# A retention layer and two gated MLPs on one core: block 0's sixteen steps in a written order, state products in four quarters, weights read back permuted

## The chip, the core and the metric

The kernel runs on one core of one Trainium2 chip. The metric is device time of one execution in microseconds (us), as the median of several runs. TensorE does the matmuls, VectorE, ScalarE and GpSimd the elementwise work, SyncE issues the transfers. In the profile they are PE, DVE, ACT, POOL and SP, and PEld is the loading of weights into TensorE. All matmuls of this kernel write PSUM, which is organised in banks of 512 fp32 columns for each partition.

## The reference

Three stages follow each other. A retention layer (batch 2, 8 heads, 768 positions, head size 64) keeps one 64x64 state for each head. Its output, as 1536 tokens of 512 features, goes through a gated MLP with 2048 hidden features, and then through a normalised second MLP with 1536. Weights and inputs are given in double precision.

```python
def _attn_ref(q, k, v):
    gamma = 1.0 - 2.0 ** (-5.0 - np.arange(H, dtype=np.float32))
    for t in range(S):
        state = gamma[None, :, None, None] * state + np.einsum('bhd,bhe->bhde', k[:, :, t], v[:, :, t])
        y[:, :, t] = scale * np.einsum('bhd,bhde->bhe', q[:, :, t], state)

def _moe_ref(x, w_in, w_out):
    h = x @ w_in
    g = h * (1.0 / (1.0 + np.exp(-1.702 * h)))
    return g @ w_out

def _moe2_ref(x, w_gate, w_val, w_out, rms_g):
    rms = np.sqrt(np.mean(x * x, axis=-1, keepdims=True) + 1e-06)
    xn = x / rms * rms_g
    g = xn @ w_gate
    silu = g * (1.0 / (1.0 + np.exp(-g)))
    val = xn @ w_val
    return silu * val @ w_out
```

## The kernel before

**Tokens and blocks.** The 1536 tokens are three blocks of 512, each of four chunks of 128 positions, so the retention layer has twelve chunks, 0 to 11, with a new batch at chunk 6. An opening computes chunks 0 to 3, which are the tokens of block 0. Then a loop of sixteen steps f runs the first MLP for block 0, 128 hidden features a step, and fits the retention of chunks 4 to 11 between. After it, blocks 1 and 2 go through the first MLP together, by seven products for each pair of steps in the manner of Strassen (`m0` to `m7`, L712), and the second MLP follows.

**A weight's way.** A weight tile w arrives as double words. One conversion turns it into fp32: two ScalarE copies (L162, L163), and on VectorE a shift (L166), a sum on 16-bit words (L167) and the sign (L173), each needing the one before. Every matmul operand of the MLPs is split into a high half (a rounded copy on ScalarE, L387 or L420) and a low half (the difference, on VectorE, L388 or L421), and a product is three matmuls. The names end in h and l: `wih`, `wil` for the input weights, `gh`, `gl` for the gate; `wo` holds both halves of an output weight. Converted input weights are also stored to memory (`wm0d` and so on, two steps in a tile), output weights as halves (`wo0d`), and `reload` (L189) reads the former back for blocks 1 and 2, 512 KB in one transfer.

**A step.** Step f does the twelve matmuls of h (L405, `mlp1_in`), one visit to the retention, the gate g (L427, L420, L421) and the twelve matmuls `acc` of step f-1 (L382 to L384). Visits alternate between scores (L265) with their two masks (L277, VectorE) and the state visit. Steps 4 and 9 have two visits. A state visit has the inter products (L294: the state S_sb times the decayed queries, skipped where a batch begins), the intra products (L307: masked scores times values), the copy of y to x, called xr (L328, ScalarE), and, unless the batch ends, the update products u (L351) with the decay (L359, ScalarE) and the sum (L367, VectorE) of the state. Inter puts head 2n+e at rows e of the array and at partitions e of one PSUM tile y, so two of the array's four 64x64 quarters are used.

**What sets the order.** Up to the end of the opening the order of each engine is the written one (`in_order(opening)`). From there a scheduler places each engine's instructions by priority, under data dependencies; only the instructions of the first two steps (`HELD`) are kept behind the opening's last one on their engine. Loads of weights, stores and reloads go by SyncE in its order. At the end of the loop the work of blocks 1 and 2 starts: sums and splits of x (`m_tasks`, L579 and L388: `xm`, `xml`, `mt`) and of weight set 0 and 1 (`set_tasks`, L612: `swm`, parts x, y, z), placed at steps 13 to 15.

Of the kernel before, what the change touches and what calls it, by code (L numbers as in the profile page):

```python
# [18 lines left out]
C = 128  # L19
# [19 lines left out]
HELD = 2  # L39
# [6 lines left out]
def tile_retention_mlp_swiglu(  # L46
# [146 lines left out]
    def split_in(f):  # L193
        if f < F1:
            t = parts["wi", f] = [wa_p.tile([128, 512], F32R, tag=f"wa{s}", name=f"wi{s}{f}") for s in "hl"]
            halves(*t, raw["w1", f][:, 0:512].bitcast(F32))
# [4 lines left out]
    def split_out(f):  # L201
        t = wo_p.tile([128, 1024], F32R, tag="wo", name=f"wo{f}")
        parts["wo", f] = both(t)
        halves(*both(t), raw["w1", f][:, 512:1024].bitcast(F32))
# [133 lines left out]
    def attend(c, p):  # L338
        inter(c, p)
        intra(c)  # L340
        x_high(c)
        at.pop(("y", c))
# [42 lines left out]

    def halves(hi, lo, src):
        nc.scalar.activation(out=hi, in_=src, func=ACTF.Copy)  # L387
        nc.vector.tensor_tensor(out=lo, in0=src, in1=hi.bitcast(F32), op=ALU.subtract)  # L388
# [29 lines left out]
    def gate_parts(key, g):  # L418
        hi, lo = gt[key] = two_parts(key[1])
        nc.scalar.activation(out=hi, in_=g, func=ACTF.Copy, scale=1.0 / GELU)  # L420
        nc.vector.scalar_tensor_tensor(  # L421
# [3 lines left out]
    def mlp1_act(f, ps):  # L425
        g = tmp(f"g{f}")
        nc.scalar.activation(out=g, in_=ps, func=ACTF.Silu, scale=GELU)  # L427
        gate_parts(("wo", f), g)
# [447 lines left out]
    ends = in_order(opening)  # L876

    def attention(c):
        return [lambda: scores(c, ps_t), lambda: (attend(c, ps_t), state(c, ps_t), following(c))]
# [8 lines left out]
    def next_of(tasks):  # L888
        if tasks:
            tasks.pop(0)()  # L890

    att = [x for c in range(CPB, B * NC) for x in attention(c)]
# [305 lines left out]
```

## Time and profile before

| what | value |
|---|---|
| median of 3 runs | 596.02 us (595.58 to 596.24) |
| the profiled execution's own time | 594.39 us |
| its span in the trace | 592.6 us |
| TensorE busy | 584.7 us, 99% |
| VectorE busy | 450.5 us, 76% |
| ScalarE busy | 357.3 us, 60% |
| GpSimd busy | 26.1 us, 4% |
| granted TensorE clock | 1.00 in every stretch shown |

The profiled execution is one run, and its time stands beside the median. The span is what the trace covers between its first and last instruction. A busy share is an average over the whole span; what bounds a stretch is read from the timelines of that stretch. In the rows, `y<-qd,S_sb` says which tile is written from which; in square brackets stands how long the engine stood idle before an instruction, and what it then had been waiting for. Matmul records overlap, so their starts are compared and not their durations.

### The profile page before, as it was taken

What the parts mean: (1) busy time and instruction counts of PE and PEld (TensorE: products, weight loads), DVE (VectorE), ACT (ScalarE), POOL (GpSimd) and SP (SyncE); (2) the same over time, 40 slices, a digit from 0 to 9 for tenths busy, and PEclk for the clock granted to TensorE, in tenths of its full rate; (3) what the DMA queues carried; (4) which work ended last, traced back from release to release, by engine and by line L of the source; (5) the groups of instructions that cost most, each with busy time, mean ns of one, the idle gap of its engine ahead of it and who ended that gap; (6) DMA issues with size and microseconds to landing.
All of it is one profiled execution on the core that took longest, in us unless ns stands there. A gap on an engine that the chain in (4) does not pass through costs nothing.

```text
span 592.6 us, 9365 instructions
## 1 busy us (share of the span) xinstructions
PE 584.7 (99%) x3306; PEld 486.2 (82%) x3306; DVE 450.5 (76%) x828; ACT 357.3 (60%) x684; POOL 26.1 (4%) x28
## 2 busy tenths in 40 slices
PE   9999999999999999999999999999999999999997
PEld 6787887887788888878878888888989889988885
DVE  2999897978999786647889999987765766654542
ACT  2686767865777786536458676555554445544532
POOL 4300311000000000000000000000000000000000
PEclk9999999999999999999999999999999999999999
DMA  8989899898269888987894644736223376553521
GB/s 328 395 237 414 334 314 364 290 310 301 75 247 308 300 284 303 287 292 266 291 341 133 194 140 143 267 107 205 98 90 106 101 266 239 177 158 103 167 72 71
DMA packets 47855, 135.11 MB, mean 228 GB/s; under 512 B 5568, under 2 KB 5824, under 8 KB 47808
## 3 DMA queue, kind: packets, MB, share of 16 engines
q1 hardware_dynamic: 47376, 134.37, 66.4%
q8 instruction: 26, 0.43, 0.3%
q10 hardware_dynamic: 432, 0.14, 0.1%
q14 instruction: 21, 0.17, 0.1%
HBM read 98.84 MB, written 35.65 MB: 227 GB/s over the span
## 4 chain that ended last, share of the span: by engine, by line
PE 90%; DMA 5%; DVE 2%; ACT 2%; SPq 0%; issue 0%
PE acc L382 7%; PE h L405 7%; PE acc L384 7%; PE acc L383 6%; PE o L382 6%; PE o L383 6%; PE o L384 6%; DMA w<-in_w 2%; PE sc L265 1%; PE y L307 1%; PE y L294 1%; DMA qk<-in_qk 1%; DMA wowq<-wo11d 1%; PE g2a L712 1%; PE v2a L712 1%; PE g10a L712 1%
## 5 line engine op out<-in xcount | busy, mean ns | idle before, releaser
L383 PE MATMUL o<-w,gh 128*128 128x512 f32 x144 | 56.2, 390 | 0.0
L384 PE MATMUL o<-w,gl 128*128 128x512 f32 x144 | 56.1, 389 | 0.0
L382 PE MATMUL o<-w,gh 128*128 128x512 f32 x144 | 55.7, 390 | 0.0
L167 DVE CUSTOM_DVE_ANT_0 qw<-qw,uw 128x1024 uint16<-128x1024 uint16 x68 | 48.2, 710 | 2.9 <-ACT uw L163 0.5
L162 ACT ACTIVATE qw<-w 128x512 f32<-128x512 f32 x68 | 45.0, 662 | 0.7 <-DMA w<-in_w 0.7
L163 ACT ACTIVATE uw<-w 128x512 uint32<-128x512 uint32 x68 | 45.3, 666 | 0.0
L166 DVE TENSOR_SCALAR qw<-qw 128x512 uint32<-128x512 uint32 x68 | 30.7, 452 | 18.2 <-ACT qw L162 18.2
L388 DVE TENSOR_TENSOR gl<-gw,gh 128x512 fp32r<-128x512 f32 x24 | 16.6, 692 | 25.7 <-ACT gh L387 25.7
L384 PEld LDWEIGHTS o<-w,gl 128*128 128x128 f32 x144 | 27.0, 188 | 5.6
L387 ACT ACTIVATE gh<-gw 128x512 fp32r<-128x512 f32 x24 | 15.1, 631 | 27.3 <-PE o L383 24.6
L382 PEld LDWEIGHTS o<-w,gh 128*128 128x128 f32 x144 | 27.1, 188 | 4.7
L383 PEld LDWEIGHTS o<-w,gh 128*128 128x128 f32 x144 | 27.1, 188 | 4.6
L382 PE MATMUL acc<-gh,wo 128*128 128x512 f32 x64 | 26.0, 411 | 0.0
L382 PE MATMUL acc<-gh,wowq 128*128 128x512 f32 x64 | 25.2, 394 | 0.6 <-ACT x L448 0.5
L382 PE MATMUL acc<-gh,wowp 128*128 128x512 f32 x64 | 24.3, 393 | 1.2 <-ACT gh L420 1.2
L384 PE MATMUL acc<-gh,wowq 128*128 128x512 f32 x64 | 25.2, 394 | 0.0
L384 PE MATMUL acc<-gh,wo 128*128 128x512 f32 x64 | 25.1, 393 | 0.0
L383 PE MATMUL acc<-gl,wo 128*128 128x512 f32 x64 | 25.1, 393 | 0.0
L383 PE MATMUL acc<-gl,wowq 128*128 128x512 f32 x64 | 25.0, 391 | 0.0
L383 PE MATMUL acc<-gl,wowp 128*128 128x512 f32 x64 | 25.0, 390 | 0.0
L384 PE MATMUL acc<-gh,wowp 128*128 128x512 f32 x64 | 24.9, 389 | 0.0
L173 DVE SCALAR_TENSOR_TENSOR qw<-w,qw 128x512 uint32<-128x512 uint32 x36 | 24.6, 684 | 0.1
(1510 smaller groups left out, 1695.9 us busy)
## 6 DMA issues: line engine op xcount, KB each, us to landing
w<-in_w SPq DMA_DIRECT2D x68, 512.0 KB, 5.7
qk<-in_qk SPq DMA_DIRECT2D x12, 512.0 KB, 8.1
kv<-in_kv SPq DMA_DIRECT2D x12, 512.0 KB, 8.4
gmd<-gm SPq DMA_DIRECT2D x16, 256.0 KB, 4.0
gwm<-gmd SPq DMA_DIRECT2D x16, 256.0 KB, 4.0
g1d<-gs SPq DMA_DIRECT2D x12, 256.0 KB, 2.4
g2d<-gl SPq DMA_DIRECT2D x12, 256.0 KB, 2.0
gw<-g1d SPq DMA_DIRECT2D x12, 256.0 KB, 2.7
```

The costliest lines, as they stand in the source:

```text
L162: nc.scalar.activation(out=q, in_=high.bitcast(F32), func=ACTF.Copy, scale=2.0 ** -112)
L163: nc.scalar.activation(out=t, in_=low, func=ACTF.Copy, scale=2.0 ** -29)
L166: lambda: nc.vector.tensor_scalar(out=m, in0=m, scalar1=3, scalar2=None, op0=ALU.logical_shift_left),
L167: lambda: nc.vector.tensor_tensor(out=m, in0=m, in1=t, op=ALU.add),
L173: nc.vector.scalar_tensor_tensor(out=dst, in0=high, scalar=0x80000000, in1=m, op0=ALU.bitwise_and, op1=ALU.bitwise_or)
L382: nc.tensor.matmul(out=out, lhsT=ah, rhs=bh, start=first, stop=False)
L383: nc.tensor.matmul(out=out, lhsT=ah, rhs=bl, start=False, stop=False)
L384: nc.tensor.matmul(out=out, lhsT=al, rhs=bh, start=False, stop=last)
L387: nc.scalar.activation(out=hi, in_=src, func=ACTF.Copy)
L388: nc.vector.tensor_tensor(out=lo, in0=src, in1=hi.bitcast(F32), op=ALU.subtract)
L405: nc.tensor.matmul(out=ps, lhsT=w[a][:, k * 128:(k + 1) * 128], rhs=x[b][:, k, :], start=o == order[0], stop=o == order[-1])
L712: nc.tensor.matmul(out=bank, lhsT=u, rhs=v, start=first and k == 0 and x == 0, stop=k == 1 and x == 2, skip_group_check=True,)
```

## The change

Four things change. First, the sixteen steps are written out in an order for all four compute engines, and that order is held to the end of the loop (`in_order(opening)` stands behind it). Of the two conversions that each step carries, the first is done inside the step; of the second, the ScalarE part stands at the end of a step and the VectorE part at the start of the next. High and low halves are issued apart (`in_high`, `in_low` and so on), and masks and state sums have written places. Second, the state visits of chunks 4 to 11 put head 2n+e at rows e and columns n%2 of the array, with the two e in two PSUM banks, `y_0` and `y_1`, so all four quarters are used; `u` moves to the other PSUM pool; the copy to x becomes two copies, `x_raw`. Third, this leaves the features of x in another order for blocks 1 and 2, so `reload` reads their input weights back in that order, as eight transfers of 64 KB, each with pieces of 512 bytes, where one of 512 KB stood. Fourth, set 0 is read back at step 11 instead of 13, and a table, `AHEAD`, says how many of the sums and splits of x and of set 0 each late step takes.

```diff
--- before.py
+++ after.py
-HELD = 2
+AHEAD = {F1 - 7: (1, 0), F1 - 5: (1, 0), F1 - 3: (0, 2), F1 - 2: (2, 2), F1 - 1: (3, 1)}
...
     def reload(kind, i):
         t = raw[kind, i] = wr_p.tile([128, 1024], F32, tag="wr", name=f"{kind}{i}r")
-        nc.sync.dma_start(out=t, in_=kept[kind, i])
+        if kind != "wm":
+            nc.sync.dma_start(out=t, in_=kept[kind, i])
+            return
+        to = t.rearrange("p (f e i c) -> p f e i c", f=2, e=2, i=2)
+        of = kept[kind, i].rearrange("p (f i s c) -> p f i s c", f=2, i=2, s=2)
+        for f in range(2):
+            for s in range(2):
+                for e in range(2):
+                    nc.sync.dma_start(
+                        out=to[64 * s:64 * s + 64, f, e], in_=of[64 * e:64 * e + 64, f, :, s]
+                    )
...
     def attend(c, p):
-        inter(c, p)
-        intra(c)
-        x_high(c)
-        at.pop(("y", c))
+
+        y = [psum(p, f"y{c}_{e}") for e in range(2)]
+        at_of = lambda n, e: y[e][64 * (n % 2):64 * (n % 2) + 64, n // 2 * C:n // 2 * C + C]
+        if c % NC:
+            qd = at.pop(("qd", c))
+            for n in range(NP):
+                for e in range(2):
+                    r = slice(64 * e, 64 * e + 64)
+                    nc.tensor.matmul(
+                        out=at_of(n, e),
+                        lhsT=S_two[(c - 1) % 2][r, n, :],
+                        rhs=qd[r, n * C:(n + 1) * C],
...
+        for e in range(2):
+            for n in range(NP):
+                nc.tensor.matmul(
+                    out=at_of(n, e),
+                    lhsT=ld["kv", c][:, 1, 2 * n + e, :],
+                    rhs=at["a", c, e][:, n * C:(n + 1) * C],
...
+    def x_raw(c):
+        for e, y in enumerate(at.pop(("y", c))):
+            nc.scalar.activation(
+                out=x_of(c)[0][:, 2 * e:2 * e + 2], in_=y[:, 0:2 * C].rearrange("p (i t) -> p i t", i=2), func=ACTF.Copy
+            )
...
-    ends = in_order(opening)
...
+    visits = deque(x for c in range(CPB, B * NC) for x in (("scores", c), ("state", c)))
+
+    def visit(what, c):
+
+        if what == "scores":
+            score_products(c, ps_t)
+            return [], [lambda: masks(c)]
+        attend(c, ps_t)
+        last = c % NC == NC - 1
+        if not last:
+            update_products(c, ps_h)
+        following(c)
+        if last:
+            return [lambda: x_raw(c)], []
+        return [lambda: x_raw(c)], [lambda: decay(c), lambda: add_update(c)]
...
     for f in range(F1):
-        begun = len(nc.cur_bb.bb.instructions)
-        while f and count["converted"] < min(2 * f + 4, 2 * F1):
-            convert_next()
-        split_out(f)
-        if f:
-            split_in(f + 2)
-        if f == F1 - 3:
+        twice = f in (4, 9)
+        if f == F1 - 5:
             start_set(0)
         if f == F1 - 2:
             phase.close()
             later["wb"] = side(ctx, "wb", 3)
             later["gs"] = side(ctx, "gs", 3)
-            mops = deque(m_tasks())
             start_set(1)
-            some(mops, 1)
-            some(sets[0], 1)
-        if f == F1 - 1:
-            some(mops, 4)
-            some(sets[0], 3)
+        if f:
+            in_high(f + 1)
+        run(rest)
+        if f:
+            in_low(f + 1)
+        if f < F1 - 2:
+            rest = convert_next(split=True)
+        out_high(f)
         ps = mlp1_in(f)
-        next_of(att)
-        mlp1_act(f, ps)
-        if f == 0:
-            convert_next()
-            split_in(2)
-        if f < HELD:
-            for x in nc.cur_bb.bb.instructions[begun:]:
-                if x.engine in ends:
-                    after(x, ends[x.engine])
+        copies, sums = visit(*visits.popleft()) if visits else ([], [])
+        g = mlp1_act(f, ps)
+        if twice:
+            run(sums)
+        if f < F1 - 2:
+            run(rest)
+            load_next()
+        gate_low(("wo", f), g)
+        out_low(f)
+        if not twice:
+            run(sums)
+        rest = []
+        if f < F1 - 1:
+            rest = convert_next(split=True) + [load_next]
+        run(copies)
+        if f in AHEAD:
+            some(mops, AHEAD[f][0])
+            if f > F1 - 5:
+                some(sets[0], AHEAD[f][1])
         if f:
             mlp1_out("wo", 0, f - 1)
-        if f in (4, 9):
-            next_of(att)
-    assert not att
+        if twice:
+            copies, sums = visit(*visits.popleft())
+            run(copies)
+            run(sums)
+    assert not visits
+    in_order(opening)
```

TensorE at chunk 4's state visit, before. `S_sb` is the state, `qd` the decayed queries, `a` the masked scores, `kv` keys and values:

```order
L294 MATMUL y_499<-qd_399,S_sb_100 64x128 x8
L307 MATMUL y_499<-a_0_431,kv_154 64x128
L307 MATMUL y_499<-a_1_433,kv_154 64x128
...
L351 MATMUL u_518<-kv_154,kd_401 64x64 x8
```

The same place after, with the line numbers of the changed kernel (L370 inter, L380 intra, L403 update):

```order
L370 MATMUL y_0_488<-qd_399,S_sb_100 64x128
L370 MATMUL y_1_489<-qd_399,S_sb_100 64x128
...
L380 MATMUL y_0_488<-a_0_451,kv_154 64x128 x4
L380 MATMUL y_1_489<-a_1_453,kv_154 64x128 x4
L403 MATMUL u_506<-kv_154,kd_401 64x64 x8
```

The inter products now alternate between two banks, and intra does all of the first mask `a_0` before the second, `a_1`.

VectorE at steps 0 and 1 before, where `w` is a converted weight, `qw` its working tile and `a` a masked score:

```order
L173 SCALAR_TENSOR_TENSOR w_286<-w_64_147,qw_385 128x512
L277 TENSOR_TENSOR a_0_431<-sc_0_421,dm_sb 128x512
L277 TENSOR_TENSOR a_1_433<-sc_1_422,dm_sb 128x512
L388 TENSOR_TENSOR wo_403<-w_286,wo_403 128x512
L166 TENSOR_SCALAR qw_442<-qw_442 128x512
L421 SCALAR_TENSOR_TENSOR gl_438<-g_435,gh_437 128x512
```

The same place after:

```order
L173 SCALAR_TENSOR_TENSOR w_286<-w_64_147,qw_385 128x512
L166 TENSOR_SCALAR qw_406<-qw_406 128x512
L167 ISA qw_406<-qw_406,uw_407 128x1024
L173 SCALAR_TENSOR_TENSOR w_405<-w_64_149,qw_406 128x512
L486 SCALAR_TENSOR_TENSOR gl_438<-g_435,gh_437 128x512
L442 TENSOR_TENSOR wo_410<-w_286,wo_410 128x512
L300 TENSOR_TENSOR a_0_451<-sc_0_425,dm_sb 128x512
L300 TENSOR_TENSOR a_1_453<-sc_1_426,dm_sb 128x512
```

The masks moved behind a whole conversion, a gate's low half and an output weight's low half.

TensorE behind block 0 after, from the last products of the y part of set 0 to the first gate of blocks 1 and 2 (`wm0y`, `wm0z`, `wm1x`, `wm1y` are parts of weight sets 0 and 1, `xmh`, `xml` halves of a sum of x):

```order
L778 MATMUL m1b<-xmh_1470,wm1xl 128x512
L778 MATMUL m1a<-xmh_1753,wm1yh 128x512
L778 MATMUL m0b<-xmh_1758,wm0zh 128x512
...
L778 MATMUL m1a<-xml_1754,wm1yh 128x512
L434 MATMUL acc_0_1922<-gh_1837,wowp_1841 128x512
```

Before, the first matmul with `wm1yh` stood behind all of the first gate's products:

```order
L712 MATMUL m1b<-xmh_1687,wm1xl 128x512
L382 MATMUL acc_0_1878<-gh_1795,wowp_1799 128x512
...
L384 MATMUL acc_3_1881<-gh_1795,wowp_1799 128x512
L712 MATMUL m1a<-xmh_1695,wm1yh 128x512
```

The matmul that needs `wm1yh` moved ahead of the z part of set 0 and of that gate's products.

## Rows read from the trace of the kernel before

**Rows 1.** The page: busy time by engine, and the chain that ended last

```profile
PE 584.7 (99%) x3306; PEld 486.2 (82%) x3306; DVE 450.5 (76%) x828; ACT 357.3 (60%) x684; POOL 26.1 (4%) x28
PE 90%; DMA 5%; DVE 2%; ACT 2%; SPq 0%; issue 0%
```

**Rows 2.** Waits of TensorE: line, releaser, us in total, times, longest

```profile
PE acc L382 <- ACT gh L420: 1.2, 1, 1.2
PE m0a L712 <- ACT wm0yh L387: 0.4, 1, 0.4
```

**Rows 3.** Stretches: busy PE, PEld, DVE, ACT, POOL, clock, DMA share, GB/s

```profile
30.00:60.00 30.00, 30.00 (x234) 23.99 (x234) 27.88 (x49) 22.85 (x42) 1.91 (x3) 1.00 0.93 329
60.00:130.00 70.00, 70.00 (x527) 56.41 (x526) 63.10 (x104) 50.94 (x98) 11.45 (x9) 1.00 0.92 323
...
140.00:150.00 10.00, 8.91 (x38) 6.60 (x36) 9.99 (x20) 7.74 (x14) 0.00 (x0) 1.00 0.58 207
```

**Rows 4.** Timeline of TensorE, state visits of chunks 4 and 5: start, us, instruction

```profile
30.11 1.09 PE L294 MATMUL y<-qd,S_sb 64*64 64x128 f32 x16
31.13 1.09 PE L307 MATMUL y<-a,kv 128*64 128x128 f32 x16
32.06 0.64 PE L351 MATMUL u<-kv,kd 128*64 128x64 f32 x16
32.62 0.50 PE L382 MATMUL acc<-gh,wo 128*128 128x512 f32 x1
...
46.21 1.09 PE L307 MATMUL y<-a,kv 128*64 128x128 f32 x16
```

**Rows 5.** Timeline of VectorE at steps 0 and 1

```profile
28.12 0.69 DVE L173 SCALAR_TENSOR_TENSOR w<-w,qw 128x512 uint32<-128x512 uint32 x1
28.73 1.28 DVE L277 TENSOR_TENSOR a<-sc,dm_sb 128x512 f32<-128x512 f32 x2
...
34.40 0.42 DVE L166 TENSOR_SCALAR qw<-qw 128x512 uint32<-128x512 uint32 x1
...
36.30 0.42 DVE L166 TENSOR_SCALAR qw<-qw 128x512 uint32<-128x512 uint32 x1
```

**Rows 6.** Timeline of ScalarE at step 0

```profile
30.42 0.62 ACT L420 ACTIVATE gh<-g 128x512 fp32r<-128x512 f32 x1
```

**Rows 7.** Timeline of TensorE at the end of block 0 and behind

```profile
138.63 0.84 PE L382 MATMUL acc<-gh,wo 128*128 128x512 f32 x3
...
143.85 0.39 PE L712 MATMUL m0b<-xmh,wm0xl 128*128 128x512 f32 x1
144.63 0.50 PE L712 MATMUL m0a<-xmh,wm0yh 128*128 128x512 f32 x1 [0.39 <-ACT wm0yh L387]
...
148.91 0.39 PE L712 MATMUL m1b<-xmh,wm1xl 128*128 128x512 f32 x1
150.52 0.96 PE L382 MATMUL acc<-gh,wowp 128*128 128x512 f32 x3 [1.21 <-ACT gh L420]
```

**Rows 8.** Timeline of VectorE at the end of block 0

```profile
131.97 0.69 DVE L421 SCALAR_TENSOR_TENSOR gl<-g,gh 128x512 fp32r<-128x512 f32 x1 [1.33 <-ACT gh L420]
...
133.75 1.23 DVE L388 TENSOR_TENSOR xml<-xr,xmh 128x1024 fp32r<-128x1024 f32 x1
134.89 1.22 DVE L579 TENSOR_TENSOR mt<-xr,xr 128x1024 f32<-128x1024 f32 x1
...
142.82 0.76 DVE L612 TENSOR_TENSOR swm<-wm0r 128x256 f32<-128x256 f32 x2
```

**Rows 9.** Set 4's reload: first use, issue; landings: two kinds, KB each, us

```profile
L612 DVE TENSOR_TENSOR swm<-wm4r x2: 418/421/424, 166.5 to 166.9; 128x256 f32<-128x256 f32 x2
L189 SPq DMA_DIRECT2D wm4r<-wm4d x1: 423/423/423, 162.0 to 162.0; - x1
...
g2d<-gl SPq DMA_DIRECT2D x12, 256.0 KB, 2.0
wm4r<-wm4d SPq DMA_DIRECT2D x1, 512.0 KB, 4.5
```

More of the change, by code (lines that the diff above doesn't have):

```diff
@@ L194, in split_in, with in_high, in_low, out_high @@
         if f < F1:
+            in_high(f)
+            in_low(f)
+    def in_high(f):
+        if f < F1:
             t = parts["wi", f] = [wa_p.tile([128, 512], F32R, tag=f"wa{s}", name=f"wi{s}{f}") for s in "hl"]
-            halves(*t, raw["w1", f][:, 0:512].bitcast(F32))
+            high(t[0], raw["w1", f][:, 0:512].bitcast(F32))
+    def in_low(f):
+        if f < F1:
+            low(*parts["wi", f], raw["w1", f][:, 0:512].bitcast(F32))
     def both(t):
         return t[:, 0:512], t[:, 512:1024]
-    def split_out(f):
-        t = wo_p.tile([128, 1024], F32R, tag="wo", name=f"wo{f}")
+    def out_high(f):
+        t = raw["wo", f] = wo_p.tile([128, 1024], F32R, tag="wo", name=f"wo{f}")
         parts["wo", f] = both(t)
-        halves(*both(t), raw["w1", f][:, 512:1024].bitcast(F32))
+        high(both(t)[0], raw["w1", f][:, 512:1024].bitcast(F32))
+    def out_low(f):
+        t = raw.pop(("wo", f))
+        low(*both(t), raw["w1", f][:, 512:1024].bitcast(F32))
         kept["wo", f] = tc.dram_tile([128, 1024], F32, name=f"wo{f}d")
@@ L384, in product, with high, low @@
         nc.tensor.matmul(out=out, lhsT=al, rhs=bh, start=False, stop=last)
+    def high(hi, src):
+        nc.scalar.activation(out=hi, in_=src, func=ACTF.Copy)
+    def low(hi, lo, src):
+        nc.vector.tensor_tensor(out=lo, in0=src, in1=hi.bitcast(F32), op=ALU.subtract)
     def halves(hi, lo, src):
-        nc.scalar.activation(out=hi, in_=src, func=ACTF.Copy)
-        nc.vector.tensor_tensor(out=lo, in0=src, in1=hi.bitcast(F32), op=ALU.subtract)
+        high(hi, src)
+        low(hi, lo, src)
     def two_parts(f):
@@ L418, in gate_parts, with gate_high, gate_low @@
     def gate_parts(key, g):
+        gate_high(key, g)
+        gate_low(key, g)
+    def gate_high(key, g):
         hi, lo = gt[key] = two_parts(key[1])
         nc.scalar.activation(out=hi, in_=g, func=ACTF.Copy, scale=1.0 / GELU)
+    def gate_low(key, g):
+        hi, lo = gt[key]
         nc.vector.scalar_tensor_tensor(
@@ L427, in mlp1_act @@
         nc.scalar.activation(out=g, in_=ps, func=ACTF.Silu, scale=GELU)
-        gate_parts(("wo", f), g)
+        gate_high(("wo", f), g)
+        return g
     def mlp1_item(key, j, f, m):
@@ L886, in following @@
             prep(c + 1)
[L888 to L892, printed above, removed]
     sets = {}
@@ L901, in some, with run @@
             tasks.popleft()()
-    for f in range(F1):
-        begun = len(nc.cur_bb.bb.instructions)
-        while f and count["converted"] < min(2 * f + 4, 2 * F1):
-            convert_next()
-        split_out(f)
-        if f:
-            split_in(f + 2)
-        if f == F1 - 3:
+    visits = deque(x for c in range(CPB, B * NC) for x in (("scores", c), ("state", c)))
[11 more added lines that the diff above has]
+        return [lambda: x_raw(c)], [lambda: decay(c), lambda: add_update(c)]
+    def run(tasks):
+        for t in tasks:
+            t()
+    for c in (CPB, 2 * CPB):
+        x_of(c)
+    mops = deque(m_tasks())
+    rest = []
+    for f in range(F1):
+        twice = f in (4, 9)
+        if f == F1 - 5:
             start_set(0)
```

12 lines of the change are left out of this document (10 added, 2 removed).

## The prediction, made before the changed kernel had run

> **What bounds the kernel now.** I read four views in this order. First the page: TensorE is busy 584.7 us, 99% of the span, VectorE 76%, ScalarE 60%, and the chain that ended last is 90% TensorE [rows 1]. So an edit counts only if it changes TensorE's own work or lets TensorE wait. Second, TensorE's waits: the two that the change touches are one of 1.2 us for a gate's high half and one of 0.4 for the high half of a weight sum [rows 2]. Third, the windows: TensorE is full from 30 to 130 us, while block 0's steps run, and loses 1.09 us of the ten just behind them; VectorE is busy 27.88 of 30 us early in block 0, 63.10 of the next 70, and 9.99 of 10 behind it [rows 3]. Fourth, the timelines of TensorE, VectorE and ScalarE at the two places that the change reorders. What a reader should see: inside block 0 there is no wait to remove, so only less matmul time gains there; VectorE has little room at its start, so an order held by hand can cost there; and the two waits near 144 and 150 us are where something else can be won.
>
> **The state products.** One visit of the inter products takes 1.02 us, 30.11 to 31.13, with 16 records [rows 4]. Before, only the diagonal quarters of the array are used (rows e with columns e), so the records run as eight pairs. After, the order goes round all four quarters: four groups of four. The intra products behind them, also 16 records, take 0.93, 31.13 to 32.06 [rows 4]. I estimate from the two that a pair costs 0.11 and that about 0.15 of the inter visit is the change of the array's mode, which stays. Four groups instead of eight then save 4 x 0.11 = 0.44 a visit. Bounds: update's 16 records take 0.56, 32.06 to 32.62 [rows 4], so the engine can bring in and use 16 sets of weights in that time at least, and if this is the limit a visit saves 0.88 - 0.56 = 0.32. From below, the saving is zero if the quarters do not run together (a rival). I take 0.44, nearer to the pair's price. Seven visits in the sixteen steps have such products (chunks 4, 5, 7, 8, 9, 10, 11; chunk 6 starts a batch): 7 x 0.44 = **-3.1 us**, with -2.2 as the bound if they run by four.
>
> Before's rows already have both diagonal quarters writing one bank, y, at the pace of pairs. The Trainium skill's page "TensorEngine Tiling (Array Packing)", section "Tiling Modes", counts four independent tiles in the 64 by 64 mode; its section "Restrictions and Gotchas" says that different row tiles cannot use one PSUM bank simultaneously. By the first the gain is the one summed here, by the second alone before's diagonal could not have run by pairs at all; no row of before shows four at once.
>
> The copies of y to x become two of 128x256 instead of one of 128x512 for each chunk, on ScalarE, busy 22.85 of 30 us here [rows 3]. TensorE needs x only in block 1, so I cost them at nothing; without that cover it is a fraction of a 512-wide copy for each of eight chunks.
>
> **The written order, where it begins.** In before, VectorE ends w_286 at 28.73 and goes straight to chunk 4's two masks, 1.20 us for both [rows 5]; the intra products start at 31.13 and wait for nothing [rows 4]. In after, VectorE has one whole conversion (three operations, each needing the one ahead), gl_438 and wo_410 between w_286 and the masks. A conversion by itself takes 34.40 to 36.30 = 1.9 [rows 5]; a 512-wide operation 0.6, as a mask does. The gate's gh starts at 30.42 [rows 6], so gl has it by then. Thus 28.73 + 1.9 + 0.6 (gl) + 0.65 (wo) = 31.9 for the start of the masks, 32.5 and 33.1 for their ends. With the shorter inter products intra could begin at 30.7; its second half needs the second mask, so it ends at 33.1 + 0.47 = 33.6, update adds 0.56, and the acc matmuls of step 0 start at 34.2 instead of 32.62 [rows 4]: **1.6 us late**, with chunk 4's gain already inside. TensorE itself waits about 2.0. Bounds: with the conversion's three operations at 0.4, 0.6 and 0.6 it is 1.3 late; with 0.3 to 0.5 of ScalarE's delay for gh or the copies it is 2.1.
>
> From there six visits give 6 x 0.44 = 2.6, so block 0 ends at 1.6 - 2.6 = **-1.0**. I walked the next places by the same durations: chunk 5's masks end at about 46.1, and its intra products, at 46.21 before [rows 4], come to 46.21 + 1.6 - 0.44 = 47.4, so 1.3 us are in hand; later masks have 2.5 us and more. VectorE's work for two steps is about 12.8 us (four conversions at 1.6 to 1.9, two masks, a state sum, two gl, four low halves at 0.6 to 0.65) against some 14.6 of TensorE, so it gains on it step by step.
>
> **The written order, where it ends.** Before, matmuls follow one another at 0.227 (23 of them from 138.63 to 143.85), but the next comes 0.78 later, and the one behind 148.91 comes 1.61 later: 0.55 + 1.38 = 1.93 us are lost [rows 7]. The table AHEAD moves sums and splits of blocks 1 and 2 into steps 13 to 15. In after VectorE goes from the gl of step 14 (131.97 before [rows 8], so about 130.9) to the last sum of weight set 1 without a gap: thirteen 512-wide operations at 0.6, seven 1024-wide at 1.14 (133.75 to 134.89) and seven 256-wide at 0.38 [rows 8] make 7.8 + 8.0 + 2.7 = 18.5, so the sum is there at about 149 and its half wm1yh some 0.6 later, less what starts early; I take 149.1. TensorE's step 14 ends at 138.63 - 1.0 = 137.6, and it has 42 matmuls before the first that needs wm1yh: 42 x 0.227 = 9.5, so it gets there at 147.1. One wait of about **2.0** stands where two lost 1.93. I take -0.1 for this place, since what is queued behind the wait is then ready. Bounds: -1.9 (no wait) to +1.5 (the 18.5 with 0.05 more on each operation).
>
> **Weights read back permuted.** Each reload of 512 KB becomes eight pieces of 64 KB with rows of 512 B. Set 4's reload is issued at 162.0, lands in 4.5 and is first used at 166.5 [rows 9]. No row shows a 64 KB piece. From above: eight after one another at 2.0, the shortest landing of a 256 KB transfer on the page [rows 9], are 16 us. From below: they go together in 4.5. I take 5 to 6, nearer to the lower end, because the transfer engines are at 0.58 in the stretch behind block 0 [rows 3] and the pieces are in flight together. SyncE issues seven more transfers for a reload, 0.42 each [rows 9], so 3.0 us later for the last. VectorE would wait about 1 us for sets 3 and 4 at a time when it waits for TensorE anyway: **0**, and up to 1 if that cover is gone.
>
> The Trainium skill's page "DMA: Bandwidth & Descriptors", section "Rules for kernel authors", speaks against this edit: transfers to disjoint halves of the partitions serialize, one over 128 partitions is better, and under 64 KB one pays mostly overhead. What that would do is the last rival; no row here shows it.
>
> **Sum.** -1.0 (block 0) - 0.1 (its end) + 0 (reloads) = -1.1 us on the profiled execution of 594.39: 593.3. The median of the runs, 596.02, lies 1.63 above that run; the same distance puts the forecast at **594.9 us**.
>
> **Rivals.**
> *The waits are smaller than walked.* If the lateness at step 0 is 1.3, or the wait for wm1yh shrinks or goes because sums were done early, the gain is 1.4 to 3.0, **593.0 to 594.6**, and with both 592.7. For it: before's VectorE stands idle 1.33 us ahead of 131.97 [rows 8], which after fills. Against: after that its list has no gap.
> *Quarters run only two at a time.* The 3.1 is not there: **598.0**. For it: every row of before shows pairs. Against: the pairs are already tiles with other rows and other columns. It decides where an inter visit stays at 0.9 us or more.
> *Held order makes VectorE late* (the other side): each chunk's masks stand behind a whole conversion, a gl and a low half, and an instruction that waits for ScalarE holds all behind it, where before the masks went ahead. If a step costs VectorE 0.7 more than I walk, two steps cost 14.2 to 14.6, the 1.3 in hand at chunk 5 is used up in two steps, and then some seven visits each let TensorE wait 0.3 to 0.6: +2 to +4 less 1.1, **597 to 599**. It decides from 14.6 us of VectorE for two steps.
> *The reloads land late.* Pieces one after another: 16 us instead of 5. Sets 3 to 5 then hold VectorE, and TensorE behind it, 2 to 4 us each: +4 to +9, **599 to 604**.
> That the change doesn't do what it says: its instructions name four quarters and the pieces, so what stays open is only whether they run together, the second and last rival.
>
> **How the numbers follow.** Forecast (594.0 to 595.9) 0.40; smaller waits 0.25; quarters by twos 0.12; VectorE late 0.13; reloads late 0.10. 0.2%, about what a measurement of this kernel can tell from no change, is 1.2 us, so 594.8 parts faster from same, in the middle of the forecast's own range: 0.20 to each side. Faster: 0.20 + 0.25 = 0.45. Same: 0.20 + 0.05 of the mildest slower cases = 0.25. Slower: 0.30. The range, 591.8 to 599.5, reaches from both waits gone with a little more to the low end of late reloads, and leaves out about 0.15.
>
> **What would show it.** An inter visit of 0.55 to 0.65 us is right, near 1.0 is quarters by twos. A wait of intra for a mask between 31 and 33 us, and acc of step 0 at 34.2; then no TensorE wait until 140; one wait of about 2 us near 147 for wm1yh; reloads that land in 5 to 8 us and no TensorE wait between 151 and 260. Masks that hold up later chunks, or waits for set halves behind 155 us, would prove me wrong.

## The result, and the profile after

The changed kernel takes 603.97 us as the median of 4 runs (602.61 to 606.73) against 596.13 before; the ratio is 1.0138 (95% interval 1.0096 to 1.0180). It is 8 us slower where 1 us less was forecast. Its profiled execution is the longest of the four: 606.73 us, span 604.9. TensorE's own work is not longer (584.4 us busy; 584.7 before, [rows 1]); the time went into waits, and into matmuls at a lower granted clock. All waits of TensorE over 0.5 us behind the opening that [rows 2] don't have, from the list of waits (line, releaser, sum in us, times, longest):

```profile
PE y L370 <- DVE a L300: 3.3, 1, 3.3
PE m0b L778 <- ACT g L492: 2.4, 1, 2.4
PE acc L434 <- DMA wowp<-wo10d: 2.1, 1, 2.1
PE acc L434 <- DMA wowp<-wo13d: 1.9, 1, 1.9
PE m1a L778 <- ACT wm1yh L439: 1.6, 1, 1.6
...
PE acc L434 <- DMA wowq<-wo11d: 0.9, 1, 0.9
```

The busy times by stretch (columns as in [rows 3]; the third from the right is the granted clock, 1.00 being 2.4 GHz) show where: TensorE was full in the first of these stretches before, and the clock is below 1.00 in the first three. The fourth holds the waits for `wowp`, of 2.1 and 1.9 us, and its clock is 1.00.

```profile
30.00:60.00 30.00, 26.57 (x192) 21.11 (x191) 25.58 (x41) 22.17 (x45) 4.31 (x4) 0.94 0.91 312
140.00:150.00 10.00, 7.59 (x30) 5.82 (x29) 8.91 (x14) 5.12 (x8) 0.00 (x0) 0.90 0.62 186
150.00:160.00 10.00, 8.36 (x34) 6.52 (x33) 9.25 (x17) 6.84 (x13) 0.00 (x0) 0.93 0.66 226
200.00:260.00 60.00, 57.94 (x256) 47.68 (x255) 43.54 (x81) 40.85 (x76) 0.00 (x0) 1.00 0.87 288
```

A ledger helps with so many waits. Every kernel here has the same matmuls in blocks 1 and 2, so I count matmuls from the last one and set the start of each against its start in the profile of before. The table gives this lateness in us, for the matmul that before starts at the time in the head, in the profiled execution of each kernel. The experiments' names are explained below.

| kernel | 25 | 36 | 130 | 165 | 260 | 350 | median, us | ratio to before (95%) |
|---|---|---|---|---|---|---|---|---|
| the change | 0.7 | 5.8 | 3.3 | 7.9 | 12.2 | 12.4 | 603.97 | 1.0138 (1.0096 to 1.0180) |
| e1_masks_first | -0.2 | 0.9 | -0.2 | 4.3 | 8.3 | 7.5 | 604.15 | 1.0144 (1.0121 to 1.0168) |
| e2_last_conversion | -0.2 | 4.9 | 2.0 | 4.2 | 8.3 | 10.6 | 603.85 | 1.0142 (1.0118 to 1.0165) |
| e3_one_reload | -0.2 | 4.9 | 1.9 | 5.8 | 5.8 | 9.7 | 601.82 | 1.0112 (1.0083 to 1.0140) |
| e4_quarters_only | 0.3 | -0.1 | -0.3 | 4.2 | 4.2 | 7.9 | 600.42 | 1.0073 (1.0046 to 1.0099) |
| e6_quarters_one_reload | -0.1 | -0.5 | -0.9 | -0.9 | -0.9 | -1.3 | 595.06 | 0.9982 (0.9960 to 1.0005) |
| e7_pieces_only | -0.1 | 0.0 | 0.5 | 4.4 | 4.4 | 5.3 | 600.05 | 1.0062 (1.0036 to 1.0087) |
| e8_held_order_only | -0.1 | 4.9 | 4.3 | 7.6 | 7.6 | 10.1 | 603.01 | 1.0104 (1.0074 to 1.0135) |
| e9_heads_swapped | 0.1 | 0.1 | -0.5 | 0.0 | 0.0 | 0.2 | 595.50 | 0.9995 (0.9972 to 1.0018) |
| e10_three_mended | 0.0 | 1.1 | 0.3 | 1.0 | 1.0 | 0.9 | 597.15 | 1.0008 (0.9979 to 1.0038) |
| e11_filled_wait | - | 3.4 | 2.9 | 5.6 | 5.6 | 6.8 | 600.98 | 1.0070 (1.0043 to 1.0098) |
| e12_swapped_held_visit | 0.1 | 0.1 | -0.2 | -0.2 | -0.2 | 0.1 | 595.04 | 0.9971 (0.9948 to 0.9994) |
| e13_whole_row_pieces | 1.0 | 3.3 | 2.9 | 15.8 | 29.7 | 30.4 | 623.08 | 1.0430 (1.0372 to 1.0488) |
| e14_other_bank | -0.1 | 2.8 | 2.3 | 5.7 | 5.7 | 5.9 | 603.15 | 1.0119 (1.0082 to 1.0156) |
| e15_queries_later | 0.3 | 4.5 | 3.9 | 7.3 | 7.3 | 8.6 | 602.42 | 1.0104 (1.0070 to 1.0138) |

How to read it: the change loses 5 us between 25 and 36 (chunk 4), gains 2.5 until 130 (the quarters), loses 4.6 at the end of block 0, and 4.3 more until 260. One execution of each kernel was traced, and executions of one kernel differ: e8's four by 3.7 us, before's by up to 6.8 in one set. The change's traced execution is the longest of its four and before's is 1.7 below its median, so the 12.4 of the last column stands against 7.8 between the medians. A single place is read from a profile, and a total from medians and intervals.

Chunk 4's state visit on TensorE (start, us, instruction, and in brackets the wait ahead of it), to set beside [rows 4]:

```profile
34.31 1.17 PE L370 MATMUL y<-qd,S_sb 64*64 64x128 f32 x16 [3.32 <-DVE a L300]
35.41 1.98 PE L380 MATMUL y<-a,kv 128*64 128x128 f32 x16
37.17 1.07 PE L403 MATMUL u<-kv,kd 128*64 128x64 f32 x16
```

Inter itself waits for the mask, and then everything is slow: inter to intra 1.10, intra to update 1.76 where [rows 4] have 0.93. The granted clock of these stretches:

```profile
34.00:35.30 1.30, 0.88 (x16) 0.61 (x16) 1.16 (x4) 0.15 (x1) 0.00 (x0) 1.00 0.84 132
34.00:36.00 2.00, 1.58 (x22) 1.20 (x24) 1.83 (x5) 0.15 (x1) 0.00 (x0) 0.84 0.76 164
36.00:38.00 2.00, 2.00 (x30) 2.00 (x26) 1.86 (x4) 1.28 (x3) 0.00 (x0) 0.50 1.01 379
38.00:40.00 2.00, 2.00 (x13) 1.58 (x10) 1.97 (x4) 2.00 (x7) 0.00 (x0) 0.81 0.78 193
```

A clock of 0.50 is 1.2 GHz. It explains the 1.76, but not the 1.10 of inter: to 35.30 the clock is 1.00. Two records of inter start at 34.31 and 34.44, the third only at 34.82, when the second mask has ended (33.48 + 1.28 = 34.76); `y_1` takes the bank of the second score. VectorE and GpSimd ahead of the visit, to set beside [rows 5]:

```profile
30.07 1.56 DVE L167 CUSTOM_DVE_ANT_0 qw<-qw,uw 128x1024 uint16<-128x1024 uint16 x1
...
33.48 1.28 DVE L300 TENSOR_TENSOR a<-sc,dm_sb 128x512 f32<-128x512 f32 x2
```

```profile
29.73 1.36 POOL L261 TENSOR_TENSOR qd<-qk,qd_sb 128x512 f32<-128x512 f32 x1 [2.35 <-DVE w L173]
```

The conversion's sum takes 1.56 us and not 0.69: a GpSimd product was under way beside it (29.73 to 31.09). Before, the same product ran beside the two masks, and these took their 1.28 us all the same [rows 5]:

```profile
28.94 1.30 POOL L238 TENSOR_TENSOR qd<-qk,qd_sb 128x512 f32<-128x512 f32 x1 [2.35 <-DVE w L173]
```

So the new order put another VectorE operation beside this product. Later visits are as forecast, 0.60 us from inter to intra and no wait (chunk 10):

```profile
111.51 0.67 PE L370 MATMUL y<-qd,S_sb 64*64 64x128 f32 x16
112.11 1.09 PE L380 MATMUL y<-a,kv 128*64 128x128 f32 x16
113.03 0.63 PE L403 MATMUL u<-kv,kd 128*64 128x64 f32 x16
```

The end of block 0 on TensorE, then on ScalarE (beside [rows 7]):

```profile
147.05 0.50 PE L778 MATMUL m0b<-xmh,wm0xh 128*128 128x512 f32 x1 [2.41 <-ACT g L492]
...
157.62 0.50 PE L778 MATMUL m1a<-xmh,wm1yh 128*128 128x512 f32 x1 [1.65 <-ACT wm1yh L439]
```

```profile
145.88 0.63 ACT L439 ACTIVATE wo<-w 128x512 fp32r<-128x512 f32 x1 [4.77 <-DVE w L173]
146.42 0.58 ACT L492 ACTIVATE g<-h 128x512 f32<-128x512 f32 x1
```

m0b takes the bank of step 15's h, which is free once ScalarE has read it as g. That g had its h early; it stood behind the high half of wo 15, which waited 4.77 us for the last conversion, which VectorE had behind the sums that AHEAD moved there. Last, SyncE's queue (beside [rows 9]: one reload, one issue of 0.42):

```profile
219.12 6.73 SPq L197 DMA_DIRECT2D wm7r<-wm7d  x8
...
227.56 0.42 SPq L234 DMA_DIRECT2D wowp<-wo10d  x1
```

The eight pieces hold the queue for 6.73 us, and the output weight issued behind them is the one for which TensorE then waits 2.1.

### The profile page after: what moved, and what is told of

It reads as the page before. It is cut to its first block, busy times and chain, and to the rows that moved or that the text cites. A ratio compares the mean times of both kernels' runs of the same rounds, so it can differ in the third digit from the quotient of the medians.

```text
span 604.9 us, 9453 instructions
## 1 busy us (share of the span) xinstructions
PE 584.4 (97%) x3306; PEld 484.7 (80%) x3306; DVE 455.5 (75%) x828; ACT 358.5 (59%) x692; POOL 26.0 (4%) x28
## 4 chain that ended last, share of the span: by engine, by line
PE 78%; DMA 9%; DVE 8%; ACT 3%; issue 1%; SPq 0%; DVEq 0%; ACTq 0%
PE acc L434 6%; PE o L435 5%; PE o L434 5%; PE o L436 5%; PE acc L435 5%; PE acc L436 5%; PE h L463 4%; DMA w<-in_w 3%; DVE qw L167 1%; DVE w L173 1%; DMA wowp<-wo13d 1%; DMA qk<-in_qk 1%; DMA wowq<-wo11d 1%; DMA wowp<-wo10d 1%; PE y L380 1%
## 5 line engine op out<-in xcount | busy, mean ns | idle before, releaser
L167 DVE CUSTOM_DVE_ANT_0 qw<-qw,uw 128x1024 uint16<-128x1024 uint16 x68 | 51.2, 753 | 5.1 <-ACT xr L392 0.5
L439 ACT ACTIVATE wo<-w 128x512 fp32r<-128x512 f32 x16 | 10.1, 631 | 30.5 <-DVE w L173 30.5
L434 PE MATMUL acc<-gh,wowp 128*128 128x512 f32 x64 | 23.9, 394 | 3.9 <-DMA wowp<-wo10d 2.1
L173 DVE SCALAR_TENSOR_TENSOR w<-w,qw 128x512 uint32<-128x512 uint32 x32 | 24.6, 767 | 1.0
```

The lines of the kernel that those rows point to most:

```text
L167: lambda: nc.vector.tensor_tensor(out=m, in0=m, in1=t, op=ALU.add),
L173: nc.vector.scalar_tensor_tensor(out=dst, in0=high, scalar=0x80000000, in1=m, op0=ALU.bitwise_and, op1=ALU.bitwise_or)
L434: nc.tensor.matmul(out=out, lhsT=ah, rhs=bh, start=first, stop=False)
```

## The experiments

The experiments come in four sets. First one suspected cause taken out of the changed kernel at a time.

**e1_masks_first.** The `run(sums)` of step 0 moved ahead:

```diff
-        if twice:
+        if twice or f == 0:
             run(sums)
         if f < F1 - 2:
             run(rest)
...
-        if not twice:
+        if not (twice or f == 0):
             run(sums)
```

> The changed kernel with one move: in step 0 the two masks of chunk 4 stand ahead of the conversion on VectorE. Theory (chunk 4's inter products wait for the masks, since y_0 and y_1 take the two banks of the scores, and the wait lowers the clock behind it): inter follows h of step 1 without a wait, intra takes 0.93 us again and not 1.76, acc of step 0 starts some 4.5 to 5 us earlier against the opening's end, the time falls by 4 to 5 us, to about 599. Rival (the wait is for something else, the state or the queries, and the masks only came last by chance): the wait shrinks by no more than 1 us, time 603. Rival (the low clock has nothing to do with the wait): the wait goes but intra keeps 1.7 us: time down by 3 us only.

Measured: chunk 4's wait is 0.5 us, intra 0.92, block 0 runs at 1.00, and between 25 and 36 the kernel loses 1.1 us and not 5.1. But the median stays (604.15): the losses at the end of block 0 and for wowp are all there, and at 36 a new one of 1.3 came in step 1 (in it, h of step 2 waits 0.5 for g, since u now lies in its pool). So the place is right, and the total doesn't show it. (The traced execution of e1, 602.22, is the shortest of its four, and that of the change the longest, so the ledger flatters e1.)

**e2_last_conversion.** In step 14 the rest of the conversion runs ahead of the table's sums:

```diff
         run(copies)
+        if f == F1 - 2:
+            run(rest)
+            rest = []
         if f in AHEAD:
```

> The changed kernel with one move: the VectorE part of the last conversion stands at the end of step 14, ahead of the sums of blocks 1 and 2, and not behind them. Theory (m0b waits for the bank of h15, which ScalarE's g15 frees, and g15 stands behind the high half of wo 15, which waits 4.8 us for that conversion): the wait of 2.4 us at m0b goes, g15 follows h15 at once, time down by 2 to 4 us, to about 601. Rival (VectorE is simply full here, the wait moves to wm1yh or to the last acc): time within 1 us of the changed kernel's.

Measured: the wait of m0b is gone, and so is the one for wm1yh; the stretch from 130 to 165 loses 2.3 us and not 4.6. In its place the last acc waits 1.4 for gh and 0.9 for gl. Half of the loss there was this conversion; the median doesn't move.

**e3_one_reload.**

```diff
     def reload(kind, i):
         t = raw[kind, i] = wr_p.tile([128, 1024], F32, tag="wr", name=f"{kind}{i}r")
-        if kind != "wm":
-            nc.sync.dma_start(out=t, in_=kept[kind, i])
-            return
...
+        nc.sync.dma_start(out=t, in_=kept[kind, i])
```

> The changed kernel with each reload as one transfer of 512 KB, so the input weights of blocks 1 and 2 come back unpermuted and the product of blocks 1 and 2 is of other numbers; all instructions else are the same. Theory (the eight pieces hold up SyncE's queue, so wowp comes late and TensorE waits 2.1, 1.9 and 0.9 us for it in the profiled run, and less in the runs at 602.6): those waits go, reloads land in 4 to 8 us with one issue of 0.4 us, time about 601.5 to 602.5 with little spread. Rival (the pieces cost nothing, the late wowp comes from the 8 us that block 0 lost): the waits stay, spread stays 602 to 607.

Measured: no wait for wowp, and nothing lost from 165 to 260 where the change loses 4.3. The median is 2.2 below the change. Some of it comes back behind 260: acc waits 2.0 for ScalarE's copy of x, which stands behind a gate that is read back from memory. SyncE's whole list is earlier here: set 7's reload is issued at 179.9 and `wowp<-wo10d` at 206.9, where the change has 219.1 and 227.6. How much of that is the time of the issues and how much the order that the scheduler chose for eight transfers is not separated by any run.

**e4_quarters_only.** The kernel before with the new `attend`, `x_raw` and `reload`:

```diff
-        return [lambda: scores(c, ps_t), lambda: (attend(c, ps_t), state(c, ps_t), following(c))]
+        return [lambda: scores(c, ps_t), lambda: (attend(c, ps_t), x_raw(c), state(c, ps_h), following(c))]
```

> The kernel before, with its scheduler's order, and only the four quarters, the two banks for y, the two copies to x and the permuted reload in eight pieces. Theory (the quarters gain 0.42 a visit as seen, the loss is in the held order): six or seven visits of 0.60 us, time 593 to 594, 2.5 to 3 us below before. Rival (two banks for y next to the two of the scores make inter wait for masks whatever the order): inter waits in some visits, time 595 to 597. Rival (the pieces cost): TensorE waits behind 150 us, time 597 to 600.

Measured: 600.42, nearest to the last rival. Visits take 0.60, but there is a wait of 3.7 us for wm0yh at the end of block 0. So the loss isn't the held order's alone, and the three parts had to be taken one by one.

The second set does one part alone. **e6_quarters_one_reload** is e4 with before's `reload`; **e7_pieces_only** is before with the new `reload`; **e8_held_order_only** is the change without the other two:

```diff
     def attend(c, p):
+        inter(c, p)
+        intra(c)
...
-            update_products(c, ps_h)
+            update_products(c, ps_t)
...
-            return [lambda: x_raw(c)], []
+            return [lambda: (x_high(c), at.pop(("y", c)))], []
```

> The quarters in the kernel before's own order, with each reload as one transfer, so the input weights of blocks 1 and 2 come back unpermuted and their products are of other numbers. Theory (the quarters gain, and in the run with the pieces SyncE's eight issues of 0.6 to 1 us each made set 0 land late and VectorE's sums with it): the wait of 3.7 us for wm0yh shrinks to 0.4 to 0.7, reload issues take under 1 us again, time 593 to 594.5, below before. Rival (the quarters' two banks and u beside h make new waits that eat the gain): TensorE waits for masks or for a bank in block 0 as in the run with pieces (0.9 and more), block 0 ends no more than 0.5 us early, time 595.5 to 597.

> The kernel before with only the reload changed to eight pieces with 512-byte rows; the features of x are in their old order, so the products of blocks 1 and 2 are of other numbers. Theory (the pieces hold SyncE 5 to 8 us a reload, set 0 comes 2 to 3 us late to VectorE, and later gates and weights queue behind): reload landings 5 to 8 us, a wait for wm0yh of 2 to 4 us, waits behind 260 us for gates read back; time 599 to 601. Rival (the eight pieces are hidden, the loss comes from the order): time 595.5 to 596.5.

> The changed kernel's held order for the sixteen steps with the kernel before's state visits (one bank y, diagonal quarters, one copy, u in its old pool) and each reload as one transfer. Theory (the held order loses by itself: masks behind a conversion at step 0, g15 behind the high half of wo 15): a wait for the mask of chunk 4 of about 2 us, the wait of m0b for g of about 2.4 us with a low clock behind each; time 600 to 602. Rival (the order only loses together with two banks for y): block 0 ends as before, time 596 to 598.

Measured: the quarters alone give -1.1 us (0.9982, the interval just reaches 1), the pieces alone +3.7, the held order alone +6.2; together 8.8, where all three have 8.2, within the intervals. In e6 the long waits of TensorE are those of before, and 0.9 of the 2.9 us that seven visits save are left at 130, since TensorE waits up to 0.2 and 0.3 us for masks and gl, and in chunk 7 the scheduler put intra between the inter products (inter 68.15, intra 68.73, inter 69.09, intra 69.68). In e7 the same wait as in e4 is there:

```profile
148.65 0.79 PE L722 MATMUL m0a<-xmh,wm0yh 128*128 128x512 f32 x1 [3.67 <-ACT wm0yh L397]
```

while set 0's first half starts only 0.6 us later than before (132.4 and 131.8). VectorE shows why:

```profile
133.77 0.43 DVE L398 TENSOR_TENSOR wm0zl<-wm0r,wm0zh 128x256 fp32r<-128x256 f32 x1
138.23 1.23 DVE L398 TENSOR_TENSOR xm<-xr,xm 128x1024 fp32r<-128x1024 f32 x1 [4.03 <-ACT xm L397]
```

With eight transfers to place the scheduler gave VectorE the split xm here, where before had xml and mt [rows 8]; it stands 4 us for it, and the sums come late. So in e7 most of the pieces' cost at this place came from an order that they changed, and not from their landing; my theory for e7 had the size right and the way wrong. In e8 the wait at chunk 4 is again 3.3, with one bank for y.

**e9_heads_swapped** keeps features in order: for chunks 6 to 11 the heads of odd pairs change places on the rows (queries, keys, masks, decays, state), so all quarters are used and each head's y lands on its own partitions.

```diff
+    def half(c, n, e):
+        return e ^ (n % 2) if c >= NC else e
...
+        y = [psum(p, f"y{c}_{s}") for s in range(2)]
+        at_of = lambda n, e: y[n % 2][64 * e:64 * e + 64, n // 2 * C:n // 2 * C + C]
...
+                        out=at_of(n, half(c, n, r)),
```

> A version that has the four quarters without any permuted weights: for chunks 6 to 11 the two heads of every other pair change places on the rows of queries, keys, masks, decays and state, so each head's y lands on its own partitions; chunks 4 and 5 keep the diagonal; order, reload and the rest as the kernel before. Theory (quarters gain 0.42 a visit, five visits, if no weight transfer pays for it): visits of 0.60 us in chunks 7 to 11, time 593.5 to 595. Rival (two banks for y and u beside h make TensorE wait): time 596 to 598.

Measured: 595.50, the same as before. Block 0 gains 0.5 us, with one visit split as in e6, and 0.5 is given back at once by a longer wait for wm0yh (0.9).

The third set tests whether the causes are complete, the clock, and a better version.

**e10_three_mended** has the edits of e1, e2 and e3 together.

> The changed kernel with the three suspected causes mended together: the masks of chunk 4 ahead of the conversion, the last conversion ahead of the sums of step 14, and each reload as one transfer, so the weights of blocks 1 and 2 come back unpermuted and their products are of other numbers. Theory (these three are all the loss that matters; each alone was covered by the other two or by a wait that moved): no wait over 1.5 us in block 0 or at its end, no late wowp, time 595 to 598. Rival (the held order loses all along, in many places): time stays over 600 with new waits in the tail or for gates read back behind 260 us.

Measured: 597.15, clock 1.00 in every stretch, 1.0008 of before (0.9979 to 1.0038). Taking all three out gives back 6.8 of 7.8 us, where each alone gave 0 to 2 in the median. The ledgers explain a part of this: 2.3 and 3.9 us come back behind 260 in e2 and e3. In e1 nothing comes back there, and the later losses are as large as in the change and not larger, so why its median stays is not shown.

**e11_filled_wait** is e8 with work for TensorE while it waits:

```diff
+        if f == 1:
+            acc[0] = [psum(ps_a, f"acc0_{i}") for i in range(KD)]
+            for _ in range(12):
+                nc.tensor.matmul(out=acc[0][3], lhsT=one(128), rhs=one(T), start=True, stop=True)
```

> The kernel of the held order alone (603.0 us) with twelve extra bf16 matmuls of 512 columns into a bank that is not yet in use, put between h of step 1 and the state visit of chunk 4, so TensorE is busy for some 2.7 of the 3.3 us for which it waits there. Nothing waits for them. Theory (the granted clock falls because TensorE stood still, and costs about 1.5 us behind the wait): the granted clock of 30 to 60 us goes from 0.94 to 1.00, intra takes 0.93 us and not 1.65, update 0.56 and not 1.0, acc of step 0 starts 1.3 to 1.6 us earlier, time about 601.5. Rival (the slow intra and update come from something else): they stay as they are and the time is 603 or more.

Measured: 600.98, 2.0 below e8. The masks come when they came, but the visit runs as in [rows 4], at a clock of 1.00:

```profile
33.56 1.09 PE L307 MATMUL y<-qd,S_sb 64*64 64x128 f32 x16 [0.70 <-DVE a L290]
34.58 1.09 PE L320 MATMUL y<-a,kv 128*64 128x128 f32 x16
35.50 0.64 PE L362 MATMUL u<-kv,kd 128*64 128x64 f32 x16
36.07 0.50 PE L393 MATMUL acc<-gh,wo 128*128 128x512 f32 x1
```

In e8 acc starts at 37.09, and at 36 of the ledger the two are 1.4 apart. So the clock that fell behind the wait cost 1.4 us on top of the wait itself. It does not fall each time: of e8's four executions the one of 600.96 us has a mean clock of 1.000, and those of 604.07 and 604.70 have 0.991 and 0.993.

**e12_swapped_held_visit** is e9 with TensorE's instructions of each such visit chained in their written order:

```diff
+            pe = [x for x in nc.cur_bb.bb.instructions[begun:] if x.engine == mybir.EngineType.PE]
+            for i, j in zip(pe[1:], pe):
+                after(i, j)
```

> The version with heads swapped on the rows (595.5 us), with TensorE's instructions of a state visit of chunks 6 to 11 held in their written order, since the scheduler put intra between the inter products in one visit and so paid the change of mode twice. Theory: all five visits at 0.60 us with one change of mode, block 0 ends 1.5 to 2 us early and not 0.55, time 593.5 to 595. Rival (what is gained in block 0 is lost behind it, since sums and gates there set the time): time 595 to 596.5.

Measured: 595.04, 0.9971 of before (0.9948 to 0.9994): a gain of 0.3%, small and just clear of the interval. Its profile is no shorter than before's, since around the double visit of step 9 TensorE waits 0.7 for a mask and 0.6 for g. It has the lowest ratio here; the interval overlaps those of e6 and e9, and one that is just clear among fourteen kernels is weak evidence.

**e13_whole_row_pieces** is before with eight pieces of sixteen whole rows:

```diff
+        for s in range(8):
+            nc.sync.dma_start(out=t[16 * s:16 * s + 16], in_=kept[kind, i][16 * s:16 * s + 16])
```

> The kernel before with each reload as eight pieces of 64 KB that are sixteen whole rows of 4 KB each, no permutation. It has the count and the size of the changed kernel's pieces without its 512-byte rows. Theory one (SyncE's time for a piece comes from the many short rows, 0.6 to 1 us each there): a piece is issued in 0.35 to 0.45 us, set 0 lands in time, time 596 to 597. Theory two (the count itself holds the queue): eight pieces take 5 us or more to issue, a wait for wm0yh of 2 to 4 us, time 599 to 600.

Measured: 623.08, outside both theories. Most issues take 0.30 to 0.42 us here (about 0.60 with 512-byte rows; single ones are longer in both), so the rows do set the price of one issue; but the eight still span 4 to 8 us, and the kernel lost 27 us. Set 4's reload, for one, was issued at 185.5, behind three stores that wait for gates, and not at 162.0 as in [rows 9]. So pieces with whole rows do harm too. The scheduler's order changed with them, and the run does not part its price from that of the count in the queue.

The last set splits chunk 4's wait, on e8.

**e14_other_bank.**

```diff
-        inter(c, p)
+        inter(c, ps_h if c == CPB else p)
```

> The kernel of the held order alone (603.0 us, inter of chunk 4 starts at 33.4 us behind a wait of 3.3) with one change: chunk 4's y lies in the other PSUM pool, where no mask has to read a score first. Theory (inter waits because y takes the bank of the first score, until its mask has read it; only intra needs the masks as data): inter starts at 30 to 31 us, and a wait of about 2 us stands ahead of intra; the two parts of the wait are then told apart; acc of step 0 about 1 us earlier, time 601 to 603. Rival (inter waits for the mask in any bank, by the order of the engine's queues): inter stays at 33 us or later.

```profile
30.08 1.09 PE L307 MATMUL y<-qd,S_sb 64*64 64x128 f32 x16
33.38 0.43 PE L320 MATMUL y<-a,kv 128*64 128x128 f32 x2 [2.21 <-DVE a L290]
```

Measured: inter starts at 30.08 and only intra waits, 2.2 us; the clock stays at 1.00 in 32 to 44, and 36 of the ledger is 2.0 less than in e8. So inter was held by the bank. The median (603.15) doesn't show the 2 us; the traced execution (600.39) is the shortest of its five. At the end of block 0 of the same trace the clock does fall, behind a wait of 2.2 for wm1yh (0.83 in 150 to 160).

**e15_queries_later.** `prep(CPB + 1)` moved from step 1 to the start of step 2.

> The kernel of the held order alone with GpSimd's product for chunk 5's queries written a step later. In the runs before, VectorE's sum on 16-bit words at 30 us took 1.56 us and not 0.69 where this product (1.36 us) began beside it. Theory (a GpSimd product holds up the VectorE operation beside it, and 0.87 of the 3.3 us of waiting come from it): that sum takes 0.7 us, chunk 4's masks end 0.8 to 0.9 us earlier, the wait is 2.4 to 2.6 us. Rival (the long sum comes from something else): it stays at 1.5 us and the wait at 3.3.

```profile
29.53 0.69 DVE L167 CUSTOM_DVE_ANT_0 qw<-qw,uw 128x1024 uint16<-128x1024 uint16 x1
...
32.11 1.28 DVE L290 TENSOR_TENSOR a<-sc,dm_sb 128x512 f32<-128x512 f32 x2
```

Measured: the sum takes 0.69 again, TensorE waits 2.5 and not 3.3. So 0.8 of the 3.3 us come from the GpSimd product. After 2.5 us of waiting the clock fell all the same (0.69 in 32 to 36).

## Why the prediction was wrong, point by point

**What bounds the kernel**: right. TensorE's work did not change, and the waits made the time.

**The state products**: right in size. A visit saves 0.42 us (0.44 forecast), the four quarters run together, and in the change the six later visits give 2.5 us from 36 to 130, where 2.6 were forecast. In before's own order the saving does not all arrive: u beside h and two banks for y beside the scores made small waits, and one visit was split, so that of seven savings 0.9 us are left in e6.

**The written order, where it begins**: this step failed. It said that inter could begin at 30.7 and only intra needs the masks, 1.6 us late; 5.1 us were lost. Three things were missing in it. Inter's y takes the bank of a score (both from a pool of two), so it stands behind the mask: e14 moves it to 30.08. The conversion takes 0.87 more beside GpSimd's product: e15 takes that away. And the clock falls behind the wait: 1.4 us in e11. The sum has no term for the granted clock at all. An estimate from the change's own rows gives 1.6 as forecast, 0.87 for the sum, about 1.0 for the two banks and about 1.6 for the clock, together the 5.1. The 1.0 is found so: with the masks as they came and no bank in the way, update could end at about 35.8, by the forecast's own durations; behind intra's start at 35.41 it could end at 36.89 (0.92 and 0.56 more). The clock makes up the rest. The bounds of that step, 1.3 to 2.1, were drawn from VectorE's rows only. The Trainium skill's page "SBUF — State Buffer", section "Who interferes with whom", says that the port pair which VectorE shares with GpSimd is an exclusive lock, and that a VectorE instruction with two inputs in SBUF contends with a GpSimd instruction that reads SBUF; the two rows of 1.56 and 0.69 us agree with it.

**The written order, where it ends**: this step failed too. It had -0.1, and 4.6 us were lost. The wait for wm1yh was forecast at 2.0 at 147 and is 1.6 at 156. The wait of m0b, 2.4, and the low clock behind it were not forecast; that it stands at 147 is luck. Its cause is of the kind that the rival on the held order named (an instruction that waits holds all behind it), but on ScalarE, and through a bank. I had followed VectorE's list at that place and not ScalarE's.

**Weights read back permuted**: the step that costed it at 0 failed; it was 3.7 alone (e7), and taking it out of the change gives 2.2 (e3). I took 0.42 for each issue, and it was 0.57 to 1.27, mostly about 0.60. From its first issue to its last landing a reload takes 7 to 14 us in the change, where I took 5 to 6. The cover that I named (VectorE waits for TensorE anyway) is not the one that counts: what stands behind the pieces on SyncE, wowp, and the order that the scheduler then chooses are. The last rival had the sum about right (599 to 604) for another reason, by luck: its cause, sets 3 to 5 that land late, is none of the long waits.

**The range** ended at 599.5 because I let the rivals stand side by side; here losses at both ends of the written order and from the reloads came together, and the two of the order had the low clock behind them.

Open: what delays the gates that are read back behind 260 us in e2, e3, e4 and e8 (2 to 4 us in the ledger), and why e1, e2, e14 and e15 don't show in their medians what their profiles show at the place they mend. One profile shows one of several outcomes: the mean clock of e14's executions goes from 0.993 to 0.997, and of e1's from 0.994 to 0.997, and the traced one has 0.997 in both.

## What to carry to other kernels

Before an order is held by hand, list for each moved instruction which PSUM bank or buffer it takes, who must release that, and what stands ahead of the releaser on its engine; data alone is not enough. A wait on TensorE of some 2 to 3 us can cost more than its length, so price it with and without the low clock behind it. A transfer cut into pieces is paid in the queue that issues it, and by what stands behind it there; look for a layout that needs no permutation, as in e9 and e12.

## What the runs showed of the hardware

- Four 64x64 quarters run together in fp32: sixteen records in 0.60 us from inter to intra, where two quarters take 1.02.
- The granted clock went to 0.50 (1.2 GHz) behind a wait of 3.3 us (e8 and the change) and fell behind one of 2.5 (e15), and not where bf16 matmuls filled the wait (e11). The length of the wait alone does not tell where: behind a wait of 2.2 for wm1yh it fell in e14 (0.83 in 150 to 160) and not in e11 (1.00), and behind one of 3.0 at 275 in e8 it stayed at 1.00.
- SyncE took 0.38 to 0.90 us (mostly 0.42) to issue 512 KB in 128 rows of 4 KB, 0.57 to 1.27 (mostly about 0.60) for 64 KB in 512-byte rows, and 0.30 to 1.57 (mostly 0.30 to 0.42) for 64 KB in sixteen rows of 4 KB.
- A VectorE sum of two operands in SBUF took 1.56 us beside a GpSimd product and 0.69 without. Two masks, with one operand in PSUM, took 1.28 us beside the same product before.
